# Retention of the later segments with one row half of TensorE for each half of the heads, and q loaded in two layouts

## The chip, the cores and the metric

The kernel runs on one core of a Trainium2 chip. Its engines are TensorE (PE in the profile; its weight loads are the row PEld), VectorE (DVE), ScalarE (ACT), GpSimd (POOL) and SyncE (SP). SP issues nearly all DMA transfers of this kernel, in order, and 16 DMA engines carry them out. The metric is the device time of one execution in microseconds (us), lower is better; a time is the median of several runs.

## The reference

Retention (a linear attention whose state decays) is followed by a feed-forward block with a gate. There are 4 batch elements, 8 heads of width 64 and 768 time steps; the rows go on as 3072 tokens of width 512, the hidden width is 1536, and all is float32.

```python
gamma = 1.0 - 2.0 ** (-5.0 - np.arange(H))
for t in range(S):
    state = gamma * state + np.einsum('bhd,bhe->bhde', k[:, :, t], v[:, :, t])
    y[:, :, t] = 1 / np.sqrt(D) * np.einsum('bhd,bhde->bhe', q[:, :, t], state)
x = y.transpose(0, 2, 1, 3).reshape(B * S, H * D)
g = x @ w_gate
out = (g * sigmoid(g) * (x @ w_val)) @ w_out
```

## The kernel before

**Segments.** The 3072 tokens are worked in four segments of 768: three chunks of 128 steps of two batch elements each. Segments 0 and 1 are the two halves of the first two batch elements, 2 and 3 of the other two. A segment has three parts: retention, the up products (gate and value, with the gate's activation), and the down product. Segment 0 has its retention at the start (L633 to L744), and its up products (L937, L919) run while the weights arrive and are converted. From segment 1 on the up products (`product`, L1088) need 7 block products in place of 8 (a Strassen-like scheme with sums of x and of the weights).

**Split operands.** Large products run on a fast matmul format that holds fewer bits, so each operand is split in three terms. `near_a` (ACT), `near_b` (DVE) and `near_c` (POOL or DVE) split weights and the hidden values; `far_a`, `far_b`, `far_c` split x and the down weights of segment 0. In the plan `w` steps split the up weights, `h` steps the hidden values, `d` steps the down weights of segment 0, `x` steps the inputs of the up products, after four sums (`sum`) on DVE.

**Stage of interest.** `down_stage` (L1199) runs the down products of segment s: 72 pieces D, one for each of the 12 hidden blocks and 6 token blocks, each of three matmuls 128x512 (L1157), adding up in PSUM banks 0 to 5, one bank for each token block. Between them stands the retention of segment s+1, made of small 64x64 float32 matmuls, all issued by one helper (`mm`, L789). Such a matmul uses a quarter of PE's array: a row half (which 64 partitions the operands lie on) and a column half (which 64 partitions of PSUM it writes). A pair p is one chunk position of both batch elements (c = 0, 1), and z counts the two halves of 64 steps of a chunk. For each pair there are four groups:

- sc: the scores of keys and queries (`scores_of`); DVE multiplies them with the decay mask (`decayed`, L812) into `att`.
- A: `low` (scores times v) and half of `old` (queries times the earlier state) for z = 0, and `grow`, which makes what the 64 steps add to the state.
- B: the rest of `old` for z = 0, and `low` and half of `old` for z = 1.
- C: the rest of `old` for z = 1, and `grow` for z = 1.

In `low`, `old` and `grow` the row half belongs to a batch element and alternates with z. Scores of pair 0 use banks 4 and 5, all else banks 6 and 7 (R0 = 6). The state is kept on DVE (`keep_state`, L894) after ACT has multiplied the old one by its decay (`decay2`, L888). ACT scales k (`scale_k2`, L824), DVE and POOL scale q in place (`scale_q2`, L816 and L401), and ACT copies the result y to `chunk_x`, eight copies of 64x128 for each z (`bring_y`, L1022). From there the sums and the splits of x for the next up products are made.

**Loads.** `load_pair` (L783, L786) brings k and q with the head's width on partitions and v and k with time on partitions, 256 KB for each batch element, to places in the tile `loads`, which the up weights (`load_unit`, L1060) use as well. `w_load` (L1133, L1136) brings the down weights. The output is scaled and stored by `finish` (L1184 to L1187).

**Order.** Nothing is scheduled by a compiler. `PLAN` is a list of steps written out, and each engine runs its instructions in the order of that list; semaphores hold a step until what it reads is there. The times in `at(...)` only matter for steps that the list does not name.

Of the kernel before, what the change touches and what calls it, by code (L numbers as in the profile page):

```python
# [17 lines left out]
P = 128  # L18
# [33 lines left out]
    A0 I0 l0:0 l1:0 A2 A1 U0:0 s0 a0:1 r1 l0:2 s1 b0:1 A4 A3 l2:1 l2:0 r0 m0 K0 S0:1 c0:1 l1:2 x0:1  # L52
    t0 s2 E1 l3:0 l3:1 m1 l2:3 C0:1 g2 V0:0 a0:0 Q2 n0:0 b0:0 l2:2 x1:2 s3 x1:1 n0:1 l4:1 l4:0 l3:2
    t1 S0:0 k2 x0:2 q3 c0:0 C0:0 o2 U1:1 m2 o3 n0:3 s4 m3 a1:1 n0:4 x2:1 l5:1 l3:3 b1:1 x2:2 x3:1
    S1:1 t2 n0:2 p0:0 q4 a1:0 x3:2 c1:1 n0:5 k3 C1:1 g3 b1:0 n1:0 v0:0 l5:0 U2:3 s5 S1:0 t3 c1:0
    C1:0 l5:2 p0:1 n1:1 u0:0 u0:1 T0:0 q5 v0:1 a2 l4:2 b2 y0:1 o5 y0:0 o4 n1:3 S2 n1:2 m5 T0:1 n1:4
    c2 m4 n1:5 x5:2 p1:0 l5:3 x5:1 p1:1 u1:0 C2 v1:0 U3:1 T0:2 x4:2 T1:0 U12:0 a3 v1:1 y1:0 x4:1
    T1:1 L b3 p0:2 a12 c12 n2:0 S3 u1:1 T1:2 b12 u0:2 U4:3 c3 Z0 n2:1 v0:2 Z1 n2:3 S12 y1:1 a4 n2:2
    p1:2 v1:2 C3 u1:2 n2:4 G2:0 y0:2 C12 G2:1 n3:0 U13:1 y1:2 n3:1 n2:5 b4 T2:0 n3:2 S4 U5:2 n3:3
    c13 T2:1 W2:0 Z12 W2:1 h0 c4 i2:1 n3:4 i2:0 G3:0 n3:5 T3:0 C4 T2:2 T3:1 U6:3 j2:0 a5 G3:1 T3:2  # L60
    j2:1 Z2 n4:0 U7:0 W3:0 i3:0 n4:1 b5 n4:2 n4:3 S5 n4:4 W3:1 i3:1 n4:5 c5 G4:0 C5 n5:0 a6 b6 a13
    l4:3 T4:0 j3:0 G4:1 n5:1 j3:1 Z3 T4:1 n5:3 i4:0 n5:2 T4:2 S6 W4:0 b13 c6 i4:1 n5:4 a7 S13 C6
    W4:1 n6:0 T5:0 U8:2 Z4 b7 U14:3 n5:5 n6:1 G5:0 j4:1 S7 C13 j4:0 G5:1 n6:2 a8 n6:3 P2 n6:4 i5:1
    c14 W5:1 i5:0 Z13 c7 j5:1 T6:0 n6:5 W5:0 a14 U9:1 U15:0 C7 T5:1 G6:0 T6:1 n7:0 T5:2 G6:1 n7:3
    n7:1 T6:2 i6:0 b8 j5:0 Z5 S8 n7:4 W6:1 b14 g4 n7:2 G7:0 i6:1 W6:0 P0 c8 S14 C8 Z6 C14 h2 a9 b9
    G7:1 j6:1 n7:5 S9 n8:0 c15 n8:3 j6:0 k5 c9 W7:1 Z14 T7:0 n8:1 C9 n8:4 U10:2 a15 n8:2 i7:1 U11:1
    W7:0 T7:1 j7:1 n8:5 i7:0 T8:0 T7:2 b15 Z7 S15 a10 n9:0 G8:0 G8:1 W8:1 i8:0 n9:3 b10 j7:0 T8:1
    n9:1 n9:2 U16:3 S10 a11 n9:4 G9:0 k4 i8:1 t4 C15 c10 C10 n9:5 W8:0 g5 n10:0 T8:2 T9:0 b11 c16
    n10:1 G9:1 Z15 j8:0 j8:1 n10:2 a16 n10:3 t5 U17:2 b16 W9:0 i9:1 T9:1 0/h0.0 T9:2 S11 Z8 W9:1 S16
    G10:1 n10:4 i9:0 C16 c11 C11 n10:5 n11:0 j9:0 Z9 G10:0 n11:3 Z16 i10:1 j9:1 a17 i10:0 W10:1 P1  # L70
    n11:4 T11:0 T11:1 1/was0.0 T11:2 n11:1 W10:0 Z11 c17 n11:2 n11:5 b17 0/h0.1 0/W0 G11:1 0/h1.0
    G11:0 j10:0 0/d0.0 h1 0/h0.2 1/sc0 j10:1 i11:0 0/h1.1 0/W1 S17 0/d1.0 i11:1 0/d0.1 1/l3 C17
    T10:0 1/dec0.0 W11:0 0/d1.1 0/d0.2 W11:1 0/h2.0 j11:0 0/D0.2 j11:1 1/k0.0 1/l4 1/dec0.1 1/q0.0
    0/D0.1 1/q0.1 0/D0.4 1/k0.1 1/l5 0/D0.0 0/h2.1 0/d1.2 0/h1.2 0/h4.0 0/W2 0/Z0 1/A0 1/y0.06
    1/new0.0 0/h4.1 1/y0.01 0/D0.5 0/D0.3 0/d2.0 1/B0 0/D1.1 0/h3.0 1/y0.03 0/D1.5 1/y0.04 0/Z1
    1/y0.02 1/y0.07 1/y0.05 T10:1 1/was0.1 1/y0.15 1/y0.00 1/y0.14 0/d2.1 0/D1.4 1/y0.12 0/d2.2
    0/D1.2 1/y0.13 0/W3 Z17 0/D1.3 0/Z2 0/d3.0 0/D1.0 0/h2.2 0/h3.1 1/C0 0/W4 T10:2 0/h3.2 0/d3.1
    0/h4.2 Z10 1/y0.16 1/l7 1/y0.17 1/new0.1 1/sum0.0 0/D2.3 0/D2.1 1/y0.10 0/h5.0 1/begin 1/sum0.1
    0/d3.2 0/h5.1 1/y0.11 0/D2.5 1/sc1 0/D2.0 0/d4.0 1/was1.0 0/D2.4 0/d4.1 0/D3.4 1/l6 1/dec1.1
    0/h5.2 1/dec1.0 0/D2.2 1/x0.2.0 0/D3.1 1/q1.1 0/d4.2 0/W5 0/D3.5 1/x0.1.0 0/h6.0 1/k1.0 0/Z3  # L80
    1/sum0.3 1/k1.1 1/sum0.2 1/x0.2.1 0/D4.5 0/D3.2 0/D3.3 0/D3.0 1/q1.0 0/Z4 0/h6.1 0/D4.0 0/D4.4
    1/x0.1.2 1/x0.1.1 1/A1 1/x0.0.0 0/d5.0 1/x0.2.2 1/y1.00 0/h6.2 1/y1.06 1/x0.0.2 1/new1.0 0/D4.2
    0/d5.1 0/d5.2 0/D4.3 0/D4.1 1/y1.07 1/y1.01 0/W6 0/h7.0 1/B1 1/x0.0.1 1/y1.04 1/y1.12 0/h7.1
    1/l9 0/d6.0 0/D5.4 0/h8.0 0/d6.1 1/y1.02 0/D5.3 0/D5.2 0/W7 0/h8.1 1/y1.05 0/d6.2 1/l8 1/l11
    0/Z5 1/y1.03 1/was1.1 0/D5.5 1/C1 0/d7.0 1/y1.16 0/d7.1 0/D6.5 0/D5.0 1/y1.17 1/y1.15 1/new1.1
    0/h7.2 1/y1.14 1/y1.11 0/D5.1 1/y1.13 1/x1.2.0 0/D6.3 0/d7.2 0/D6.4 0/Z6 1/y1.10 0/D7.3 0/h9.0
    1/sc2 0/h8.2 1/x1.2.2 0/D6.2 1/q2.1 1/k2.1 0/D7.5 0/W8 1/sum1.0 0/D6.1 1/sum1.2 1/k2.0 0/D6.0
    0/D7.1 1/x1.1.0 0/h10.0 0/h9.1 0/d8.0 0/D7.2 1/dec2.0 1/l10 1/sum1.1 1/dec2.1 0/W9 1/x1.1.1
    0/D7.0 0/d8.1 1/x1.2.1 0/Z7 1/sum1.3 1/was2.0 1/q2.0 1/x1.0.0 1/x1.1.2 0/d9.0 0/D7.4 0/d8.2
    0/h11.0 1/A2 1/new2.0 0/D8.0 1/x1.0.1 0/h10.1 0/D8.3 0/D8.2 0/d9.1 1/L0 0/D8.1 1/y2.00 0/D8.4  # L90
    1/B2 0/W10 0/d9.2 1/y2.07 1/y2.05 0/d10.0 0/D8.5 0/h9.2 1/y2.02 0/h11.1 0/D9.3 1/y2.03 0/h10.2
# [279 lines left out]
def tile_retnet_swiglu(  # L371
# [314 lines left out]
    def keep_rows():  # L686
        copy(tab[:, QDEC0:KDEC0], banks[2])
# [652 lines left out]
```

## Time and profile before

| what | value |
|---|---|
| median of 3 runs | 642.69 us (641.97 to 642.97) |
| profiled execution, first to last instruction | 640.5 us |
| retention of segment 0 and first up products | 0 to 46 us |
| up products of segment 0 | 46 to 127 us |
| down of 0 with retention of 1 | 127 to 197 us |
| up of 1; down of 1 with retention of 2 | 197 to 282; 282 to 350 us |
| up of 2; down of 2 with retention of 3 | 350 to 435; 435 to 503 us |
| up of 3; down of 3 | 503 to 589; 589 to 637 us |
| small matmuls (L789) in the chain | 6.0% of the span |
| granted clock of TensorE | 1.000 |

The span is the profiled execution's own time from its first to its last instruction; what a run needs around it is the difference to the median. A group row of the profile gives line, engine, operation, the tiles written and read, shapes and count, then the busy time and the mean of one in ns, then the engine's idle time just before such instructions and what ended it. The chain is followed back from the last instruction to what released each.

### The profile page before, as it was taken

Reading aid. Unit: us, or ns where it says so; the run is one execution under the profiler, and the core shown is the slowest. Engines: PE = TensorE matmul, PEld = TensorE weight load, DVE = VectorE, ACT = ScalarE, POOL = GpSimd, SP = SyncE. Lnnn points to the kernel's source line nnn. Section 1 sums busy time; section 2 is a strip of 40 time slices with the busy share of each in tenths; the row PEclk is TensorE's granted clock in tenths of the full one; section 3 lists DMA queues with packets and bytes.
Section 4 is the critical chain, followed back from the end, with each engine's and each line's share of the span. In section 5 each row is a group of like instructions: output and inputs, shape, how many; then the busy total and the mean of one; then the engine's idle time right before and its main releaser. Section 6 shows DMA issues by size and latency. Waiting matters only on the chain.

```text
span 640.5 us, 14132 instructions
## 1 busy us (share of the span) xinstructions
PE 632.9 (99%) x5587; PEld 580.4 (91%) x5587; DVE 484.1 (76%) x715; ACT 394.3 (62%) x868; POOL 261.1 (41%) x172
## 2 busy tenths in 40 slices
PE   7999999999999999999999999999999999999997
PEld 6899999987779999997778999998777999999886
DVE  4998787899898887665797869575789866768361
ACT  4787797777865565566766555564785555654221
POOL 1534445544425866630003665550101666663000
PEclk9999999999999999999999999999999999999999
DMA  9899998798787445258765640457776444304564
GB/s 320 291 332 326 376 329 269 268 326 305 266 285 278 168 148 173 75 179 260 247 239 214 211 152 15 175 196 246 226 258 248 154 164 173 116 1 151 194 214 148
DMA packets 50626, 139.60 MB, mean 218 GB/s; under 512 B 5120, under 2 KB 18176, under 8 KB 50560
## 3 DMA queue, kind: packets, MB, share of 16 engines
q1 hardware_dynamic: 49984, 137.92, 62.6%
q8 instruction: 44, 0.72, 0.5%
q10 hardware_dynamic: 576, 0.79, 0.3%
q14 instruction: 22, 0.18, 0.1%
HBM read 108.80 MB, written 29.88 MB: 217 GB/s over the span
## 4 chain that ended last, share of the span: by engine, by line
PE 97%; DMA 3%; SPq 0%; DVE 0%; ACT 0%; issue 0%
PE bank L1088 41%; PE bank L1157 32%; PE bank L919 13%; PE bank L789 6%; PE bank L937 3%; DMA hT<-in_v_n_dram 2%; PE bank L744 1%; DMA hT<-in_q_t_dram 1%; PE bank L730 0%; PE bank L715 0%; PE bank L633 0%; DVE chunk_x L1178 0%; SPq L513 0%; ACT chunk_x L1180 0%; SPq L466 0%
## 5 line engine op out<-in xcount | busy, mean ns | idle before, releaser
L1157 PE MATMUL bank<-oitem,gitem 128*128 128x512 f32 x867 | 208.2, 394 | 0.0
L1157 PEld LDWEIGHTS bank<-oitem,gitem 128*128 128x128 f32 x867 | 159.6, 188 | 34.5 <-DVE tmp L812 0.4
L997 POOL TENSOR_TENSOR gitem<-gitem 128x768 fp32r<-128x768 f32 x71 | 138.7, 1963 | 117.9 <-DVE gitem L994 99.0
L1088 PE MATMUL bank<-xa,gitem 128*128 128x384 f32 x864 | 160.5, 334 | 0.0
L1088 PEld LDWEIGHTS bank<-xa,gitem 128*128 128x128 f32 x864 | 150.8, 188 | 0.2
L997 POOL TENSOR_TENSOR oitem<-oitem 128x256 fp32r<-128x256 f32 (+1 forms) x60 | 64.1, 1074 | 56.8 <-DVE oitem L994 48.3
L1088 PE MATMUL bank<-xb,gitem 128*128 128x384 f32 x432 | 84.5, 334 | 0.0
L919 PE MATMUL bank<-xa,oitem 128*128 128x384 f32 x480 | 84.3, 335 | 0.0
L919 PEld LDWEIGHTS bank<-xa,oitem 128*128 128x128 f32 x480 | 83.0, 188 | 0.4 <-ACT tmp L444 0.2
L994 DVE SCALAR_TENSOR_TENSOR gitem<-gitem,loads 128x768 fp32r<-128x768 f32 x72 | 75.1, 1057 | 9.1 <-ACT gitem L991 7.5
L1088 PEld LDWEIGHTS bank<-xb,gitem 128*128 128x128 f32 x432 | 75.9, 188 | 0.4
L991 ACT ACTIVATE gitem<-loads 128x768 fp32r<-128x768 f32 x72 | 59.6, 843 | 26.0 <-PE bank L1088 16.8
L994 DVE SCALAR_TENSOR_TENSOR gitem<-gitem,hT 128x768 fp32r<-128x768 f32 x48 | 46.1, 965 | 24.4 <-ACT gitem L991 24.4
L991 ACT ACTIVATE gitem<-hT 128x768 fp32r<-128x768 f32 x48 | 40.2, 842 | 31.4 <-PE bank L1157 29.4
L1022 ACT COPY chunk_x<-bank 64x128 f32<-64x128 f32 x144 | 36.6, 260 | 32.6 <-PE bank L789 21.3
L401 DVE SCALAR_TENSOR_TENSOR gitem<-gitem 128x768 fp32r<-128x768 f32 x49 | 49.7, 1022 | 1.3 <-DVE gitem L994 0.5
L816 POOL TENSOR_TENSOR loads<-loads,tab 128x512 f32<-128x512 f32 x9 | 13.4, 1493 | 82.1 <-PE bank L789 44.6
L1088 PE MATMUL bank<-xb,oitem 128*128 128x384 f32 x216 | 43.4, 335 | 0.0
L1088 PEld LDWEIGHTS bank<-xb,oitem 128*128 128x128 f32 x216 | 37.9, 188 | 0.3
L994 DVE SCALAR_TENSOR_TENSOR oitem<-oitem,loads 128x256 fp32r<-128x256 f32 (+1 forms) x42 | 34.5, 824 | 2.1 <-ACT oitem L991 2.1
L1105 DVE TENSOR_TENSOR hT<-bank,tmp 128x384 f32<-128x384 f32 x36 | 20.0, 555 | 20.7 <-PE bank L1088 20.4
L1103 ACT COPY tmp<-bank 128x384 f32<-128x384 f32 x36 | 17.2, 478 | 28.3 <-PE bank L1088 19.3
(118 smaller groups left out, 789.8 us busy)
## 6 DMA issues: line engine op xcount, KB each, us to landing
loads<-wup SPq DMA_DIRECT2D x36, 896.0 KB, 4.7
oitem<-wdnt SPq DMA_DIRECT2D x33, 768.0 KB, 4.4
wdnt<-oitem SPq DMA_DIRECT2D x12, 768.0 KB, 5.5
wup<-first SPq DMA_DIRECT2D x9, 896.0 KB, 6.7
rawp<-in_w_gate_dram SPq DMA_DIRECT2D x12, 512.0 KB, 6.8
rawp<-in_w_val_dram SPq DMA_DIRECT2D x12, 512.0 KB, 6.2
rawp<-in_w_out_dram SPq DMA_DIRECT2D x12, 512.0 KB, 5.7
out_dram<-chunk_x SPq DMA_DIRECT2D x21, 256.0 KB, 2.1
```

The costliest lines, as they stand in the source:

```text
L401: stt(o, x, 1.0, y, op0=mul, op1=op)
L789: nc.tensor.matmul(o, a, b, start=start, stop=True, skip_group_check=True)
L919: nc.tensor.matmul(o, w[:, a, ts(b, P)], X0[:, a, i, NC - 1 - b], start=a == b == 0, stop=a == 2 and b == NC - 1, skip_group_check=True)
L937: nc.tensor.matmul(o, w[:, a, ts(b, P)], X0[:, a, :, NC - 1 - b, ts(j, P)], start=a == b == 0, stop=a == 2 and b == NC - 1, skip_group_che ...
L991: act(o[0], x, AF.Copy, scale=CUT / FAR)
L994: stt(o[1], f32(o[0]), -FAR, x, op0=mul, op1=add)
L997: op(o[2], f32(o[0]), f32(o[1]), op=add)
L1022: copy(cx[half[i], ds(2 * h, 2), c, half[z]], y.rearrange("p (b t) -> p b t", b=2))
L1088: nc.tensor.matmul(o, w[:, a, k], x[:, a, KH - 1 - k], start=start and a == k == 0, stop=a == 2 and k == KH - 1, skip_group_check=True)
L1103: steps = (lambda: copy(p1, x), lambda: tt(c11, z, p1, op=add), lambda: act(gate, c11, AF.Silu, scale=ONE), lambda: copy(u2, x), lambda: c ...
L1105: lambda: copy(p5, wb), lambda: tt(h1, x, p5, op=add),
L1157: nc.tensor.matmul(banks[tok][:, cols], hs[f][:, a, ds(i * TH + u * P, P)], wo[f][:, a, cols], start=f == a == 0, stop=f == NF - 1 and a = ...
```

## The change

The row half now belongs to half of the heads (g = 0: heads 0 to 3, g = 1: heads 4 to 7) for `low`, `old` and `grow`, for both batch elements and both z. For this, v and k with time on partitions are loaded so that a row half holds 64 partitions of its four heads, both z side by side: four transfers of 64 partitions for each, in pieces of 1 KB. q is loaded twice: as before for the scores, and a fifth load of a pair (`w` = 4) for `old`, to the place that k of the scores had; DVE scales that copy, with a table that two transfers bring (`own_rows`). With this the products of one z stand in one group (`mix2`), so B holds what B and C held, and C is gone: three groups for a pair. The result of `grow` for the second batch element lies on the other row half, and ACT copies it over (`move_state`; `turn_state` once, for the state from segment 0). y now leaves PSUM in two copies of 128x256 for each z. k is scaled by ACT alone. The scores of pair 1 use banks 4 and 5.

A set ELSE names 45 steps that go to another engine than by default: 32 additions of the up weights' split and six of the down weights' split go from POOL to DVE, one stays on DVE, and six steps that scale the output change between ACT and DVE. The store of an output tile is a step of its own (`store`). The list is the same for its first 150 steps and in another order behind them; loads and steps of the retention stand in it by name. In the order of PE the small matmuls of segment 1 stand at: scores of 0, A0, scores of 1, B0, A1, B1, scores of 2, A2, B2; in segments 2 and 3 the scores of pair 1 follow A0 at once.

```diff
+    def either(step):
+        return both if step in ELSE else pool
...
-    spots = [loads[:, ts(i, 512)] for i in range(10)]
-    HOME = (2, 3, 4, 0, 1, 2, 3, 4, 0, 1, 4, 0)
+    homes = [loads[:, ts(i, 1024)] for i in range(5)]
+    homes += [chunk_x[:, ts(1, 1024)], tmp[:, ts(1, 1024)]]
+    HOME = (2, 3, 4, 5, 2, 0, 1, 3, 6, 0, 1, 4, 5, 0, 1)
...
     def load_pair(s, n):
+        p, w = divmod(n, 5)
+        t = homes[HOME[n]]
+        given.setdefault(p, {})[w] = [t[:, ts(c, 512)] for c in range(2)]
+        one, two = seg_chunks(s)[2 * p], seg_chunks(s)[2 * p + 1]
+        src = (k_t, q_t, v_n, k_n, q_t)[w][one : two + 1 : two - one]
+        if w < 2:
+            nc.sync.dma_start(out=two_of(t), in_=src.rearrange("c r n -> r c n"))
+            return
+        for c in range(2):
+            for g in range(2):
+                nc.sync.dma_start(
+                    out=two_of(t[half[g], ts(c, 512)]),
+                    in_=src[c, :, ts(g, 256)].rearrange("(z t) n -> t z n", z=2))
...
     def scores_of(p, own):
+        scored[p] = own
         kt, qt = ([pairs(t) for t in given[p][w]] for w in range(2))
+        for z in range(2):
+            for b in range(2):
                 for c in range(2):
+                    for g in range(2):
+                        for i in range(2):
+                            mm(banks[own + i][half[g], ds(256 * c + 128 * z + HC * b, HC)],
+                               kt[c][half[i], 2 * g + b, half[z]],
+                               qt[c][half[i], 2 * g + b, half[z]], z == b == c == 0)
     def decayed(p, i):
-        att[p, i] = (spare if p % 2 else tmp)[:, ts(i, 512)]
-        o, b = (t.rearrange("p (z n) -> p z n", z=2) for t in (att[p, i], scored[p][i]))
-        tt(o, b, lmask[:, i][:, None, :].to_broadcast([P, 2, NP * HC]), op=mul)
-    def scale_q2(p, i):
-        t = pairs(given[p][1][i])
-        (pool if i else both)(t, t, qdec, op=mul)
-    def scale_k2(p, i):
-        kd = given[p][3][i].rearrange("p (h d) -> p h d", h=H)
-        if p == 2 and i == 0:
-            pool(kd, kd, lk[:, :, None].to_broadcast([P, H, D]), op=mul)
-            return
-        for h in range(H):
-            act(kd[:, h], kd[:, h], AF.Copy, scale=lk[:, ds(h, 1)])
...
+    def state_of2(z, c, g):
+        return moved[half[g]] if c else states[half[g], z, g]
+    def move_state(z):
+        for g in range(2):
+            copy(moved[half[g]], states[half[1 - g], z, g])
+    def turn_state(i, g):
+        for c in range(2):
+            copy(states[half[g ^ c], 1, g].rearrange("p (b i) e -> p b i e", b=2)[:, :, i],
+                 states[half[i], 0, c, ds(2 * g, 2)])
+    def y_at(z, c, g, b, i):
+        return banks[R0 + g][half[i], ds(256 * z + 128 * c + HC * b, HC)]
     def low(p, z):
         for b in range(2):
+            for c in range(2):
+                for i in range(2):
+                    for g in range(2):
+                        mm(y_at(z, c, g, b, i),
+                           given[p][2][c][half[g], ds(256 * z + D * (2 * b + i), D)],
+                           att[p, i][half[g], ds(256 * c + 128 * z + HC * b, HC)], b == c == 0)
+    def old(p, z):
+        for b in range(2):
+            for c in range(2):
+                for i in range(2):
+                    for g in range(2):
+                        mm(y_at(z, c, g, b, i), state_of2(1 - z, c, g)[:, 2 * b + i],
+                           given[p][4][c][half[g], ds(256 * i + 128 * b + HC * z, HC)])
     def grow(p, z):
         for n in range(NP):
+            for c in range(2):
+                for g in range(2):
+                    own = ds(256 * z + D * n, D)
+                    mm(banks[R0 + g][half[g ^ c], ds(256 * (1 - z) + D * n, D)],
+                       given[p][3][c][half[g], own], given[p][2][c][half[g], own])
+    def mix2(s, p, z):
+        low(p, z)
+        if has_old(s, p, z):
+            old(p, z)
+        if has_new(s, p, z):
+            grow(p, z)
+    def decay2(z, g):
         for n in range(NP):
+            act(states[:, z, g, n], states[:, 1 - z, g, n], AF.Copy,
+                scale=lg[:, ds(NP * g + n, 1)])
...
-    def bring_y(z, h, i, c):
-        y = banks[R0 + c][half[h], ds((2 * z + i) * 2 * HC, 2 * HC)]
-        copy(cx[half[i], ds(2 * h, 2), c, half[z]], y.rearrange("p (b t) -> p b t", b=2))
+    def bring_y(z, r):
+        y = banks[R0 + r][:, ts(z, 256)].rearrange("p (c b t) -> p b c t", c=2, b=2)
+        copy(cx[:, ds(2 * r, 2), :, half[z]], y)
...
-        at(t + c, f"{s}/w{f}.{g}.2", lambda: near_c(it["o"][0], both if (s, f, g) == (1, 0, 0) else pool))
+        at(t + c, f"{s}/w{f}.{g}.2", lambda: near_c(it["o"][0], either(f"{s}/w{f}.{g}.2")))
...
-            at(t + b, f"{s}/d{f}.1", lambda: far_b(o(), f32(o()[2]), pool))
+            at(t + b, f"{s}/d{f}.1", lambda: far_b(o(), f32(o()[2]), either(f"{s}/d{f}.1")))
...
-        if tok % 2:
+        if (tok % 2 == 1) != (f"{s}/e{tok}" in ELSE):
             nc.vector.tensor_scalar(t, banks[tok], scale, None, op0=mul)
         else:
             act(t, banks[tok], AF.Copy, scale=scale)
-        nc.sync.dma_start(out=out[ds(row, P)], in_=t)
...
+            at(t, f"{nxt}/begin", begin_x, nxt)
             for f in range(3):
-                at(slot_at[UNITS[f]], f"{nxt}/L{f}", load_unit, f)
+                at(t, f"{nxt}/L{f}", load_unit, f)
+            for n in range(15):
+                at(t, f"{nxt}/l{n}", load_pair, nxt, n)
+            for i in range(4 if nxt == 1 else 0):
+                at(t, f"{nxt}/cv{i}", turn_state, i // 2, i % 2)
+            if nxt == 1:
+                at(t, f"{nxt}/cm", move_state, 1)
+            for p in range(L):
+                at(t, f"{nxt}/sc{p}", scores_of, p, 6 if p == 2 else 4)
+                for i in range(2):
+                    at(t, f"{nxt}/dec{p}.{i}", decayed, p, i)
+                    at(t, f"{nxt}/q{p}.{i}", scale_q2, p, i)
+                for n in range(NP):
+                    at(t, f"{nxt}/k{p}.{n}", scale_k2, p, n)
+                for z in range(2):
+                    at(t, f"{nxt}/{'AB'[z]}{p}", mix2, nxt, p, z)
+                    if has_new(nxt, p, z):
+                        for g in range(2 if has_old(nxt, p, z) else 0):
+                            at(t, f"{nxt}/was{p}.{z}{g}", decay2, z, g)
+                        at(t, f"{nxt}/new{p}.{z}", keep_state, nxt, p, z)
+                        at(t, f"{nxt}/mv{p}.{z}", move_state, z)
+                    for r in range(2):
+                        at(t, f"{nxt}/y{p}.{z}{r}", bring_y, z, r)
+                make_x(t, nxt, p, table)
```

## Prediction

> **What bounds the kernel now.** I read the busy shares first, then the chain that ended last in order of time, then busy time by stage, then the groups on VectorE (DVE) and GpSimd (POOL) inside one stage, then the transfers. A stage below is the stretch from the first small matmuls for segment 1, 2 or 3 to that segment's up products: 127 to 197, 282 to 350 and 435 to 503 us.
>
> ```profile
> span 640.5 us, 14132 instructions
> ...
> PE 632.9 (99%) x5587; PEld 580.4 (91%) x5587; DVE 484.1 (76%) x715; ACT 394.3 (62%) x868; POOL 261.1 (41%) x172
> ```
>
> TensorE (PE) is busy for all but 7.6 us, and those lie ahead of the first 20 us and behind the last matmul, where the change touches nothing. So the time is what PE's rows add up to: a step helps only if it shortens PE's own row, and hurts only if PE comes to wait. In the chain, each piece is start, length, line and number of records (a 64x64 fp32 matmul leaves two records, a 128x512 one leaves one):
>
> ```profile
> 146.84 1.09 PE bank L789 x64
> 147.94 8.39 PE bank L1157 x36
> 156.32 1.34 PE bank L789 x80
> 157.67 2.27 PE bank L1157 x9
> 159.93 1.09 PE bank L789 x64
> 161.02 2.95 PE bank L1157 x12
> 163.97 0.86 PE bank L789 x48
> ...
> 175.92 1.52 PE bank L789 x80
> 177.43 3.66 PE bank L1157 x15
> 181.09 1.40 PE bank L789 x64
> ...
> 185.48 0.39 PE bank L789 x16
> ```
>
> Two things are to be seen. From 16 to 64 records a small run grows from 0.39 to 1.09 us, 0.0146 us a record, so 0.156 us of each run is there whatever its size. Behind a small run the down products cost (8.39 - 2.27) / 27 = 0.227 us each, and 2.27 - 9 x 0.227 = 0.23 us more. **A run of small matmuls thus costs about 0.39 us for being a run.** Second, the runs at 175.92 and 181.09 are longer than their twins of the same size (1.34 and 1.09): 0.18 + 0.31 us of waiting inside them.
>
> By stage (window, length, busy time of PE, PEld, DVE, ACT, POOL, clock, DMA share, GB/s):
>
> ```profile
> 127.00:197.00 70.00, 70.00 (x981) 56.74 (x982) 64.81 (x90) 50.15 (x139) 27.14 (x18) 1.00 0.85 300
> 197.00:282.00 85.00, 85.00 (x492) 85.00 (x491) 63.77 (x98) 48.79 (x96) 56.83 (x35) 1.00 0.47 156
> 282.00:350.00 68.00, 68.00 (x974) 54.89 (x973) 51.07 (x79) 47.20 (x139) 9.96 (x6) 1.00 0.70 238
> ```
>
> Only in stage 1 is a second engine near PE: DVE with 64.81 of 70.00.
>
> **The change part by part.**
>
> *Fewer runs.* The built order of PE holds the same 4299 instructions, among them the same 1104 small matmuls, in both programs. The runs of small matmuls number 36 before (12 a stage) and 25 after (9, 8 and 8: C is gone, and in segments 2 and 3 A0 and the scores of pair 1 stand together). 11 x (0.156 + 0.23) = **4.3 us off**, all of it on the path. The records keep their price: the four 64x64 tiles are still taken in turn and each row half still keeps to its own bank; A (x80, with grow) and the scores (x64, without) fit the same 0.0146.
>
> *ACT.* Out go 144 copies of y (260 ns), 120 scalings of k (336) and 60 decays (392), 101 us by mean times count. In come 36 copies of 128x256 (376, the row of the first state's copy), 72 scalings of 128x128 (392), 120 decays of 128x64 (340, the early decay's row) and about 42 copies of state (376 at most): 98 us. ACT is 62% busy, so this costs nothing; PE hides it. Without that cover the terms cancel anyway.
>
> *POOL to DVE.* 50 additions and scalings leave POOL (the 9 of q, 3 of k, 6 of the first weights for down, 32 of the up weights); the new scaling of q, the 6 and 33 with an earlier one are on DVE. At 0.68 us for 128x512, 0.95 for 128x768 and 0.41 for 128x256 DVE gains some 36 us. In an up stage that is about 10 on 63.77 of 85: hidden. In stage 1 it is 9 x 0.68 = 6.1 us on 64.81 of 70, which would not fit, were it not for this pair of rows, the same line in two windows of that stage (127 to 141.9, then 170.2 to 186):
>
> ```profile
> L1007 DVE SCALAR_TENSOR_TENSOR oitem<-oitem 128x512 fp32r<-128x512 f32 x3 | 3.7, 1227 | 0.0
> ...
> L1007 DVE SCALAR_TENSOR_TENSOR oitem<-oitem 128x512 fp32r<-128x512 f32 x3 | 2.0, 679 | 0.0
> ```
>
> One of the first three took 2.32 us, while POOL was at a 1.77 us addition. Summed over the stage, DVE's rows are some 8.5 us above their shortest forms with 18 POOL instructions there. The change takes 10 of the 18 away, so I take 4.7 us back against 6.1 added: +1.4, which DVE's 5 us of idle time hold. I count the 0.5 us of waiting at 175.92 and 181.09 (its releasers are DVE's sums of x and splits) as **gone**, bounds 0 to 0.6.
> The Trainium skill, SBUF — State Buffer, "Who interferes with whom", says that a DVE instruction with two SBUF inputs and a GpSimd instruction that reads SBUF lock each other out for a whole instruction. The 2.32 us row agrees; by that rule DVE in stage 1 loses a wait of up to one POOL instruction (1.5 us) for each of the 10, and ends below its 64.81; by durations alone it would end at 70.9.
>
> *q loaded twice.* New on SP: 14 transfers for a pair instead of 10, and a dependence that was not there. The second layout of q goes to the place of k, so it is issued when the scores are done, and A's products with the state (`old`, L847) need it scaled. Rows, of the tile loads in stage 2 (ns least, median, most) and its issues (KB, median us to landing):
>
> ```profile
> L786 SPq DMA_DIRECT2D loads<-in_v_n_dram x4: 472/530/728, 302.7 to 322.7; - x4
> ...
> loads<-in_v_n_dram SPq DMA_DIRECT2D x4, 128.0 KB, 5.4
> ```
>
> The reload is four such half tiles (in 1 KB pieces, not 2 KB, which only the weight loads have here, 512 KB in 6.8 us; I bound the landing by 3.6 and 9.3 us, the quickest median of such halves, in stage 3, and the slowest of the tile's loads, in stage 1, and take 5.4). Last issue 1.6 us behind the scores, landed at 7.1, scaled on DVE at 7.8. Pairs 0 and 1 have over 14 us. For pair 2 the order leaves twelve, ten and fifteen down products (0.68 each) between scores and A; with the two switches and A's first 16 matmuls that is 8.9, 7.6 and 10.9 us. So in stage 2 it is late by 0.2. Behind it DVE holds three splits of x and two of h (0.35, 0.35, 1.15, 0.87, 0.87) ahead of the new state (0.72), and ACT then moves that state (0.75) for B, which stands four down products on: 13.0 against 12.3 us after the scores, **0.7 late in all**. In stage 1 the same sum gives 16.4 against 17.0, but one POOL instruction falls into it: **0.3**. Stage 3 has room. Bounds for the three: 0 and 8.
>
> *Banks and order.* Scores of pair 1 now use banks 4 and 5, which the down products of the tokens 4 and 5 need. In stage 1 two products stand between; DVE has a new state, a split and two decays to do: 6.4 against 6.65 us. I take **0.2**, bounds 0 and 1. New stores of the output wait later on SP, and the up steps of segment 0 are reordered; PE's 336 products there run at 0.174 us with no wait, and their transfers are issued within 10 us of where they were: 0.
>
> **Sum.** 640.5 - 4.3 - 0.5 + 0.7 + 0.3 + 0.2 = 636.9 us of span. The median of the runs, 642.69, is 2.2 above the span; that part lies outside it and stays: **639.1 us**.
>
> **Rivals.**
> *The reload is late by more* (12 in 100). Landing at 7.1 us, the slowest of loads in stage 2, adds 1.7 there and 0.6 in stage 1: 641.4. For it: four more issues a pair on one queue. Against: that queue mostly waits for others.
> *DVE is the bound in stage 1* (7 in 100). If fewer POOL instructions give nothing back, 64.81 + 6.1 = 70.9 us of DVE stand against 70 - 1.2 saved: 2.1 late, and the 0.5 stays: 641.7.
> *The runs do not cost what I say* (4 in 100): if the 0.39 us follows something else, such as the tile order or bank, nothing is won, and the waits give 643.4 or so.
> *Slower* (7 in 100). One mechanism: the reload behind the scores of pair 2. At the slowest landing, 9.3 us, q is scaled at 11.7 us after the scores, against 8.9, 7.6 and 10.9: 2.8, 4.1 and 0.8 late, 0.7 more at B: 8.4 us of waiting for 4.8 won, **646 us**. It decides from a landing of about 8 us on; the DMA share of 0.85 in stage 1 speaks for it, 0.70 in stage 2 less.
> *All is hidden* belongs to the forecast (70 in 100 with it): without any new wait 637.9, with 0.41 for a run 637.6.
>
> **Chances.** A measurement can tell about 0.2%, 1.3 us, from no change. Faster: the forecast and most of the first rival, 0.81. Same: the rest of it and DVE as the bound, 0.11. Slower: 0.08. The range reaches from 637.2 (no waits, dearer runs) to 642.4, past DVE as the bound.
>
> **What would show it.** 25 pieces of small matmuls in the chain, each at 0.156 + 0.0146 a record; a longer one, or a gap, names a wait. L1007-like rows near 0.68 us in stage 1 and DVE's busy time there not above 67. In stage 2, whether A2 and B2 wait, and for which: the load of q, or the state's copy. Wrong would be PE waiting for DVE all through stage 1, or PE below 98% of the span.

## The result, and the profile after

The changed kernel took **663.42 us** (median of 5 runs, 659.97 to 666.25), the kernel before 642.84 us beside it (5 runs, 641.97 to 643.80): a ratio of 1.0308, 95% interval 1.0277 to 1.0339. It is slower by 20.6 us where 3.6 us less were forecast. The profiled run took 666.25 us, with a span of 664.1; it is the slowest of the five. In two of the experiments below (e4 and e7) one execution lay over 1.5% above the fastest of its kernel; the ratio leaves it out, the median and the text's differences hold it.

The changed kernel's page: span, busy time of the engines, and the granted clock in 40 slices, in tenths.

```profile
span 664.1 us, 14143 instructions
...
PE 642.2 (97%) x5587; PEld 589.1 (89%) x5587; DVE 495.2 (75%) x760; ACT 391.7 (59%) x815; POOL 183.8 (28%) x122
...
PEclk9999999997999979999999999999899999999999
```

PE has as many matmuls as before, yet is busy 9.3 us longer, idle 14.3 us more, and granted less than the full clock around 156, 242 and 470 us. Two kinds of loss, then: waits, and matmuls at half clock.

The changed kernel by stage (window, length, busy time of PE, PEld, DVE, ACT, POOL, clock, DMA share, GB/s). The first and third are stages 1 and 2 of the prediction, the second is the up stage between them:

```profile
127.00:207.70 80.70, 75.18 (x936) 61.48 (x936) 65.52 (x102) 51.75 (x128) 11.32 (x7) 0.96 0.88 305
207.70:294.00 86.30, 82.99 (x519) 82.36 (x518) 63.65 (x99) 47.36 (x96) 45.84 (x28) 0.96 0.43 141
294.00:366.30 72.30, 71.10 (x941) 59.39 (x940) 57.90 (x90) 48.06 (x125) 0.74 (x1) 1.00 0.73 250
```

Stage 1 is 10.7 us longer. DVE is not what filled it: 65.52 us in the longer window, against 64.81 in 70.00 before.

What PE waited for between 127 and 600 us, as the profile names it (total, times, longest):

```profile
PE bank L1160 <- DMA oitem<-wdnt: 4.6, 3, 2.0
PE bank L1091 <- ACT tmp L1106: 3.3, 1, 3.3
PE bank L798 <- ACT chunk_x L1025: 1.9, 1, 1.9
PE bank L798 <- DVE states L897: 1.3, 1, 1.3
PE bank L1160 <- ACT states L889: 1.2, 1, 1.2
PE bank L922 <- DVE hT L459: 1.1, 1, 1.1
PE bank L798 <- DVE loads L414: 0.6, 1, 0.6
PE bank L1160 <- DVE tmp L820: 0.4, 1, 0.4
...
```

Before, PE waited for nothing there but the 0.5 us inside two runs. The first row is down weights that land late. The others name no load: they name a copy out of a bank (L1106, L1025), a state, a scaling. For the longest of them the loads stand one step further back. Take the 1.9 us, at 153.1 us. SP's queue ahead of it (start, length, line, transfer, count):

```profile
142.89 3.50 SPq L793 DMA_DIRECT2D loads<-in_q_t_dram  x4
...
147.12 0.38 SPq L1136 DMA_DIRECT2D oitem<-wdn  x1
```

And ACT, where the bracket is the idle time before:

```profile
153.46 0.63 ACT L1003 ACTIVATE oitem<-oitem 128x512 fp32r<-128x512 f32 x1 [3.87 <-DMA oitem<-wdn]
153.99 0.68 ACT L831 ACTIVATE tmp<-tmp,local 128x128 f32<-128x128 f32 x2
154.58 0.62 ACT L1025 COPY chunk_x<-bank 128x256 f32<-128x256 f32 x2
```

The four issues of q's second layout (L793) hold SP for 3.50 us. The weight behind them (L1136) goes out at 147.12, ACT waits 3.87 us to split it, and the copy of y (L1025) that stands two places behind on ACT comes late, so B cannot have its bank. The weight lands 6.2 us after its issue, at 153.35, with the DMA engines full (share 1.04 from 151 to 155 us), so the late issue is one part of its lateness and the transfers ahead of it are another. The longest wait, 3.3 us at 239.1 in the up stage, has a scaling in place of the split. ACT again:

```profile
237.69 0.40 ACT L831 ACTIVATE chunk_x<-chunk_x,local 128x128 f32<-128x128 f32 x1 [3.33 <-DMA chunk_x<-in_k_n_dram]
238.98 0.40 ACT L831 ACTIVATE chunk_x<-chunk_x,local 128x128 f32<-128x128 f32 x1 [0.89 <-DMA chunk_x<-in_k_n_dram]
...
241.87 0.47 ACT L1106 COPY tmp<-bank 128x384 f32<-128x384 f32 x1
```

k lands late, so its scalings (L831) are late, and behind them in ACT's order stands the copy (L1106) that frees a bank for the up products. In stage 2, at 339.3 us, the profile puts the wait of 1.2 us down to ACT's decay of the state (L889), but the step that waits is a down product (L1160), which reads no state. Its weight is the one to look at:

```profile
329.75 3.43 SPq L793 DMA_DIRECT2D loads<-in_k_n_dram  x4
333.28 0.54 SPq L1063 DMA_DIRECT2D loads<-wup  x1
333.94 1.69 SPq L1139 DMA_DIRECT2D oitem<-wdnt  x2
```

The first of the two weights (L1139), issued at 333.94 behind k's four issues, landed at 340.38, and PE's wait for that landing ended at 340.41, 0.1 us ahead of the product. So it is a late down weight too.

**Where 23.5 us went.** In the profiled run the last matmul ends at 660.59 us, before at 637.07. Behind 20 us PE has gaps of 15.5 us in all, before none. Half clock was granted for 6.83, 6.83 and 3.41 us; PE was busy for 15.7 us of that, so some 7.9 us of work were lost. The start is 1.0 later. Less the 4.3 us of the runs that went, this makes 20.1; the 3.4 left are not put down to a row. The clock's part differs from run to run: the mean granted clock was 0.987 here and 0.994 to 0.997 in the other four, which by these figures lost some 2 to 4 us to it (an estimate).

### The profile page after: what moved, and what is told of

Read it like the earlier page. It is cut to its first block, busy times and chain, and to the rows that moved or that the text cites. A ratio compares the mean times of both kernels' runs of the same rounds, so it can differ in the third digit from the quotient of the medians.

```text
span 664.1 us, 14143 instructions
## 1 busy us (share of the span) xinstructions
PE 642.2 (97%) x5587; PEld 589.1 (89%) x5587; DVE 495.2 (75%) x760; ACT 391.7 (59%) x815; POOL 183.8 (28%) x122
## 2 busy tenths in 40 slices
DMA packets 60850, 144.59 MB, mean 218 GB/s; under 512 B 5872, under 2 KB 33008, under 8 KB 60784
## 4 chain that ended last, share of the span: by engine, by line
PE 58%; DMA 4%; ACT 1%; SPq 0%; issue 0%; DVE 0%; ACTq 0%
PE bank L1091 35%; PE bank L1160 19%; DMA oitem<-wdnt 3%; PE bank L798 3%; DMA loads<-in_k_n_dram 0%; SPq L793 0%; ACT loads L831 0%; ACT states L889 0%; ACT gitem L994 0%; DVE chunk_x L1183 0%; ACT tmp L1106 0%; ACT bank L1107 0%; ACT chunk_x L1185 0%; ACT bank L1110 0%; ACT xb L1003 0%
## 5 line engine op out<-in xcount | busy, mean ns | idle before, releaser
L1160 PE MATMUL bank<-oitem,gitem 128*128 128x512 f32 x867 | 209.0, 398 | 6.2 <-DMA oitem<-wdnt 4.6
L1160 PEld LDWEIGHTS bank<-oitem,gitem 128*128 128x128 f32 x867 | 163.0, 191 | 43.0 <-DMA oitem<-wdnt 2.4
L1091 PEld LDWEIGHTS bank<-xa,gitem 128*128 128x128 f32 x864 | 152.9, 191 | 4.0 <-ACT tmp L1106 3.6
L1000 POOL TENSOR_TENSOR gitem<-gitem 128x768 fp32r<-128x768 f32 x48 | 96.3, 2016 | 175.1 <-DVE gitem L997 154.0
L1000 POOL TENSOR_TENSOR oitem<-oitem 128x256 fp32r<-128x256 f32 (+1 forms) x51 | 56.1, 1103 | 167.8 <-DVE oitem L997 149.8
L1091 PE MATMUL bank<-xb,gitem 128*128 128x384 f32 x432 | 81.8, 335 | 0.0
L414 DVE SCALAR_TENSOR_TENSOR gitem<-gitem 128x768 fp32r<-128x768 f32 x72 | 71.2, 994 | 1.9
L1107 ACT COPY tmp<-bank 128x384 f32<-128x384 f32 x36 | 17.2, 477 | 36.0 <-PE bank L1091 20.1
L889 ACT ACTIVATE states<-states,local 128x64 f32<-128x64 f32 x120 | 31.5, 335 | 1.5 <-DVE states L897 1.5
L1025 ACT COPY chunk_x<-bank 128x256 f32<-128x256 f32 x36 | 12.4, 367 | 30.4 <-DVE states L897 16.1
L1108 ACT COPY tmp<-bank 128x384 f32<-128x384 f32 x36 | 17.3, 480 | 14.1 <-PE bank L1091 14.0
```

Source lines behind the costliest of these rows:

```text
L414: stt(o, x, 1.0, y, op0=mul, op1=op)
L889: act(states[:, z, g, n], states[:, 1 - z, g, n], AF.Copy, scale=lg[:, ds(NP * g + n, 1)])
L1000: op(o[2], f32(o[0]), f32(o[1]), op=add)
L1025: copy(cx[:, ds(2 * r, 2), :, half[z]], y)
L1091: nc.tensor.matmul(o, w[:, a, k], x[:, a, KH - 1 - k], start=start and a == k == 0, stop=a == 2 and k == KH - 1, skip_group_check=True)
L1107: lambda: act(gate, c11, AF.Silu, scale=ONE), lambda: copy(u2, x),
```

## The experiments

The changed kernel is the base unless another is named; "before" is the kernel before on the same chip. **T1**: the time goes on SP's queue, in the four issues of every half-tile load, because what stands behind them, the down weights and the scalings of k and q above all, no longer fits the places that the list gives it. **T2**, the rival: the moves from POOL to DVE overload DVE. **T3**, named in the expectations from e2 on: the new list puts steps ahead of others that are due sooner, whatever the transfers cost.

**1. e1_else_off: POOL keeps its steps.**

```
-ELSE = {"0/d1.1", ... "3/w8.1.2"}
+ELSE = set()
```

> The set ELSE is empty, so 38 splits of weights go back from DVE to POOL and six scalings of the output change back between ACT and DVE; the loads, the retention and the list of steps stay those of the changed kernel (663.4 us). Theory 1 (in-order queues: the retention's half-tile loads hold SP, the down weights behind them come late, and ACT's and DVE's scalings that wait for a load hold other steps; the clock then falls to half): the gaps of PE at 153, 239, 339, 468 and 496 us stay, so 660 to 667 us, rather more than less since POOL locks DVE out again. Theory 2 (the 38 steps given to DVE overload it): most of the loss goes, 640 to 650 us, and DVE's busy time falls by about 25 us.

672.68 us, before 642.31: 1.0453 (1.0415 to 1.0491). The kernel gets 9 us slower without the moves, and PE's longest waits now end on POOL (6.8 us in three). T2 falls: the moves help. T1's 660 to 667 us were exceeded as well.

**2. e2_one_issue: one transfer a load.**

```
-        if w < 2:
+        if w < 5:
```

> v, k with time on partitions and the second q are each brought by one transfer of 512 KB in rows of 2 KB, not by four of 128 KB in pieces of 1 KB; same bytes, same places, same waits and same list. The data do not lie as the products need them, so the numbers computed in the retention differ. Theory 1: SP is free 2 to 3 us sooner behind each of the 27 loads, the down weights come sooner, and the gaps of PE of 15.5 us fall to under 6 and the half clock to under 4 us: 640 to 650 us. Theory 3 (the new list puts steps ahead of others that are due sooner, whatever the transfers cost): no gain, 660 to 666 us. Theory 2: no gain either.

648.21 us (646.94 to 652.75): 1.0100 (1.0062 to 1.0139); gaps 6.7 us, clock 1.000. With the same bytes, list and instructions 15 us are back, and no half clock is left behind the start. The weight of the gap at 153 us now goes out at 144.09, 3.0 us sooner, and lands at 149.74, 3.6 sooner. T1 holds; T3 by itself, which said no gain, falls.

**3. e3_no_reload: q's second load left out.**

```
+        if w == 4:
+            return
```

> The second load of q is left out (nine loads of four transfers), and the products of queries and the earlier state use what lies in that place (keys), so the numbers computed differ; the scaling on DVE and all else stays. If the second load of q alone is at fault (the prediction's slower rival): all gaps go, 637 to 641 us. Theory 1: the gaps where a down weight stands behind a q load on SP (468, 496 us) and the one at 187 us go, those of k behind its own wait (239, 339 us) and of the down weight behind the load at 143 us stay at least in part: 648 to 658 us. Theory 3: 660 us or more.

652.21 us: 1.0145 (1.0120 to 1.0170), gaps 9.2 us. The reload with its four issues is worth 11 us, though A and B wait little for it by name.

**4. e4_weights_first: weights ahead of the loads, twelve moves in the list** (`0/W2 > 1/l8`, `0/W3 > 1/l9` and so on).

> Twelve loads of down and up weights are put ahead of the retention's load that stood in front of them in the list, so SP issues them first; the same work. Theory 1: PE no longer waits for down weights (gaps at 153, 468, 496 and 517 us, 6.5 us and half clock twice, some 4 us), while the waits for k scaled on ACT at 239 and 339 us stay or grow, since the retention's loads are later by 0.5 us: 648 to 656 us. If the order on SP does not matter (theory 2): 660 to 667 us. If the retention's loads have no time to spare, the gaps only move to A and B groups: 658 to 668 us.

681.33 us: 1.0587 (1.0556 to 1.0618). Three of the moves (W7 ahead of l13 in two stages, W8 ahead of l14 in one) put a down weight into a place whose earlier weight has products later in the list, so that those products wait for the new weight and use it; that is the part of the computation it changes. PE waited 13.1 us for weights, up to 5.1 at a time. The experiment was ill made and speaks for neither side.

**5. e5_rows_2kb: still four issues, but pieces of 2 KB.**

```
-                    out=two_of(t[half[g], ts(c, 512)]),
-                    in_=src[c, :, ts(g, 256)].rearrange("(z t) n -> t z n", z=2))
+                nc.sync.dma_start(out=t[half[g], ts(c, 512)], in_=src[c, half[g]])
```

> The four transfers of 128 KB of each half-tile load stay, each with 64 partitions, but each row is one piece of 2 KB and not two of 1 KB: the same number of issues and bytes, half as many packets. The data do not lie as the products need them, so the numbers computed in the retention differ. If it is the small pieces that make the loads dear (on SP or in the DMA engines): most of what one transfer for each load gave (663.4 to 648.2 us) comes back, 646 to 654 us, and an issue is shorter than 0.6 us. If it is the number of issues in a row on SP: 658 to 666 us, four issues still 2.5 us.

661.91 us, before 642.72: 1.0309 (1.0281 to 1.0337), gaps 14.4 us. The small pieces (33008 packets under 2 KB in the changed kernel, 19184 here, 18176 before) are not at fault. With e2, it is the number of transfers for a load: their issues, their landings, or both.

**6. e6_z_form: four transfers over 128 partitions, the two halves as first dimension.**

```
+            for z in range(2):
...
+                    out=t[:, ds(512 * c + 256 * z, 256)],
+                    in_=src[c, ts(z, 64)].rearrange("t (g n) -> g t n", g=2))
```

> Each half-tile load is cut the other way: four transfers of 128 KB, each over all 128 partitions and one half of 64 steps, in pieces of 1 KB. Same bytes, same pieces, same layout, same count. Theory 1 (the issue's time on SP): it depends on whether an issue over 128 partitions is shorter; the 512 KB loads over 128 partitions take 0.43 us, so four would take 1.7 in place of 2.6 us: 655 to 662 us. If the pieces' landing decides, no change: 660 to 667 us.

880.99 us: 1.3706 (1.3684 to 1.3727). The issues (count, then least, median and most in ns):

```profile
L793 SPq DMA_DIRECT2D loads<-in_q_t_dram x36: 506/2491/5987, 127.1 to 701.8; - x36
```

DVE waited for these loads 82.7 us in 15 times, and where only these transfers ran, some 50 GB/s were moved at a busy share of one tenth, where 300 to 400 GB/s are seen beside that. The Trainium skill, DMA: Bandwidth & Descriptors, "Why a DMA increments its semaphore by 16 and not by 1", says that the number of DMA engines used is the largest up to 16 that divides the slowest dimension of both sides; here that is 2. The measurement agrees. For the question it is a miss: the form was worse than the one it replaced.

**7. e7_pool_queue: the half tiles issued from POOL** (`nc.sync.dma_start` becomes `nc.gpsimd.dma_start` at L793).

> All half-tile loads are issued by POOL and not by SP; the same list. Theory 1: SP does not stand still for 2.6 us or wait for the place of a load, so the down weights behind it are on time: the gaps at 153, 468, 496 and 517 us go, 6.5 us, and with them the half clock there; but POOL now waits for the places, and its splits behind that wait are late, DVE's and ACT's waits for k and q stay: 650 to 660 us. If SP's queue is not what delays: 661 to 668 us.

679.04 us: 1.0556 (1.0528 to 1.0583). POOL in order of time, and the wait of PE that comes of it:

```profile
126.09 2.35 POOL L793 DMA_DIRECT2D loads<-in_q_t_dram  x4
128.45 1.31 POOL L1000 TENSOR_TENSOR oitem<-oitem 128x512 fp32r<-128x512 f32 x1
129.67 4.71 POOL L793 DMA_DIRECT2D loads<-in_v_n_dram  x8
```

```profile
PE bank L922 <- DVE hT L459: 7.8, 1, 7.8
```

An issue takes 0.59 us on POOL too, and now holds POOL's splits. DVE is held in turn: the scaling of q that it began at 133.56, 0.68 us long by itself, took 3.80 us beside POOL's work, and the step that PE waited for (L459) stands two places behind it. Moving the issues to another queue that has work moves the stall.

**8. e8_moved: nine places of the list mended**, each weight or load that a gap named moved ahead (`0/W3 > 1/l9`, `0/W9 > 1/L1`, `2/W2 > 3/l9` and so on).

> Only the list is changed, in nine places, by PE's gaps of the changed kernel: five down weights (W3 and W9 of the first, W7 of the second, W2, W5, W7, W9 of the third stage; seven in all) stand ahead of the load that held them up on SP, wherever the products that free their place stand earlier, and ACT's scalings of k0 in the second up stage and of k2 in stage 2 stand later. Theory 3 (the list's order does not fit the transfers' times): the gaps at 153, 239, 339, 468, 496 and 517 us go, 11 us, with the half clock of 7 us twice: 644 to 652 us. If the gaps only move to the loads that now come later: 655 to 668 us.

662.85 us: 1.0311 (1.0278 to 1.0344), gaps 15.8 us. Of the six gaps that were aimed at only the one at 239 us went. The other five are there again within 4 us of their places, that at 152 us with DVE's state ahead of the copy of y in place of the weight, and gaps of 1.8 and 1.7 us have come at 180 and 275 us. Single moves did not mend the list.

**9. e9_laid_out: one transfer a load, with the data in its right layout.** Three more inputs hold v, k and q in the half-by-half order, prepared with the inputs and outside the time, so that the load needs no four parts:

```
+        src = (k_t, q_t, v_g, k_g, q_g)[w][one : two + 1 : two - one]
+        nc.sync.dma_start(out=two_of(t), in_=src.rearrange("c r n -> r c n"))
```

> The rows that the half-tile loads put together are laid out so in the inputs (three more arrays: k, v and q by halves of the heads; the other arrays of k, q, v, too, come permuted), so that every load is one transfer of 512 KB in rows of 2 KB over 128 partitions, with the data that the products need. The list is that of the changed kernel. Theory 1 (the four issues of a load hold SP): the same as with one transfer and the wrong rows, 646 to 650 us, clock 1.0, no gap of PE over 1.1 us. If the numbers themselves mattered (wrong rows cheaper): over 655 us.

648.63 us (645.33 to 652.27), before 643.18: 1.0084 (1.0046 to 1.0123), gaps 6.5 us. It agrees with e2, now with the whole computation. The issues of q's second layout in the changed kernel, and in e9:

```profile
L793 SPq DMA_DIRECT2D loads<-in_q_t_dram x32: 595/598/1350, 142.9 to 492.5; - x32
```

```profile
L791 SPq DMA_DIRECT2D loads<-in_q_g_dram x8: 368/376/1203, 141.2 to 471.9; - x8
```

Four of 0.60 us became one of 0.38. But with 11 runs fewer this kernel should have been at 643.18 - 4.3 = 638.9: 10 us are still missing.

**10. e10_before_split: the kernel before, with 16 issues for a pair in place of 10.**

```
+                n = 64 if i == 0 else 32
+                for m in range(0, P, n):
+                    nc.sync.dma_start(out=own[i][m : m + n],
+                                      in_=src[ds((m + 64 * i) % P, n)])
```

> The kernel before, with 16 issues for a pair in place of 10: the four 256 KB loads of v and k with time on partitions are cut in halves or quarters by partitions, same bytes and rows of 2 KB. That adds some 3.3 us of issuing for a pair on SP, about what the changed kernel adds (10 issues at 0.5 us against 14 at 0.6). Theory 1 in its plain form (time on SP is lost to PE in any order): PE waits in each of the three stages, 646 to 655 us. Theory 3 (the new list and the fifth load leave no room, the list of before does): 642 to 645 us.

648.23 us, before 643.18: 1.0067 (1.0038 to 1.0096), with gaps of 5.1 us where there were none. Issues alone take 5 us from a kernel whose list had no waits. They do not take 20: the list has a part in that. The down weights landed as in the kernel before (768 KB in a median of 4.6 us, against 4.5, from 127 to 600 us), so here it is SP's time.

**11 to 13. e11_fit_after, e12_fit_laid, e13_fit_early: the list put together anew** from the durations in the traces, by a count of what each engine, bank and queue has to do: e11 for the changed kernel's loads and e12 for those of e9, from step 378 on; e13 for those of e9 from step 186 on. Only `PLAN` differs.

> The changed kernel with the same steps on the same engines, the same loads (four transfers of 128 KB for a half-tile load) and the same places; only the list behind its first 377 steps is put together anew, from the durations that the traces of the changed kernel show, with 0.62 us for an issue over 64 partitions, 2 to 3.4 us and 300 to 360 GB/s for a landing. Theory 3 (the list's order against the transfers' times is at fault, there is room enough): PE's gaps behind 130 us fall from 13.5 to under 4 us and the half clock goes, 638 to 646 us. Theory 1 in its strict form (SP has no room for the issues in any order): 652 us or more.

> Every load one transfer, with the inputs laid out for it (k, v and q come in one more permutation), and the list behind its first 377 steps put together anew in the same way. Both theories: the gaps behind 130 us (5 us with the old list) go, 25 runs of small matmuls stay, so 648.6 - 5 to 6: 641 to 644 us; with the 0.6 us that PE also lost in waits too short to be listed, 640. If something else than waits costs the new scheme time (PE itself): 645 us or more.

> As e12, with the list anew from its 186th step on, so with the conversions and first up products of segment 0 as well. The gaps at 85 and 131 us (1.9 us with the old list) go too, 24 runs of small matmuls: 1.5 to 3 us less than e12, 637 to 641 us, at or below the forecast of 639.1. If the conversions of the weights have no room (DVE and POOL locking each other out): no less than e12.

671.45 us, 1.0449 (1.0428 to 1.0471); 667.77 us, 1.0384 (1.0367 to 1.0401); 662.51 us, 1.0305 (1.0290 to 1.0321). Three misses, all worse than the list they replaced. e12's splits on DVE (count, least, median, most in ns), and two waits of its stage 1:

```profile
L410 DVE SCALAR_TENSOR_TENSOR gitem<-gitem x60: 943/957/2601, 127.0 to 593.3; 128x768 fp32r<-128x768 f32 x60
```

```profile
DVE tmp L809 <- PE bank L1149: 3.6, 1, 3.6
...
PE bank L787 <- ACT local L833: 4.2, 1, 4.2
```

They show what the count lacked. A split of 0.95 us took up to 2.60 beside a POOL instruction. DVE's decay of the scores waited 3.6 us for down products in the other of banks 4 and 5, which the kernel declares as one tile. ACT's split of x waited 4.1 us for a place that a store of weights (`wup<-first`) was still reading, and PE 4.2 us for ACT.

**14 and 15. e14_apart_laid, e15_apart_after: the list anew, with these three counted**, from step 186 on; e14 with e9's loads, e15 with the changed kernel's own half-tile loads. Part of the list around the down weights (W) and the loads (l) of stage 1, other steps left out, in the changed kernel and in e15:

```
-1/A0 1/sc1 1/l8 0/d2.0 0/h3.0 1/l9 1/k1.3 1/k1.2 0/h5.0 0/W3 0/d3.0 1/k1.1 1/B0 0/W4 1/k1.0 1/A1 1/l10 0/W5 1/l11 1/l12
+1/A0 1/sc1 0/W2 1/l8 0/d2.0 1/l9 1/k1.3 1/k1.2 1/k1.1 0/W3 0/h3.0 1/k1.0 0/d3.0 1/B0 0/h5.0 0/W4 1/A1 0/W5 1/l12 0/W6
```

> As e13 (one transfer a load, the list anew from its 186th step on, same steps, engines and places), but the list now keeps POOL's instructions apart from DVE's with two inputs in SBUF, takes every PSUM bank (4 and 5 as one) as held by one engine at a time, and leaves 3.2 us and more for a landing. Theory 3 (order): DVE's busy time comes back to 545 us or less, gaps of PE behind 45 us under 5 us, 24 runs of small matmuls, 636 to 642 us. Theory 1 in its strict form has no say here. If the order leaves no room even so (DVE, with 38 more steps, too full beside POOL): 648 us or more.

> The same kind of list for the changed kernel with its own loads (four transfers of 128 KB for each half-tile load): only the order differs from the changed kernel (663.4 us), from its 186th step on. Theory 3 (order alone): 636 to 645 us, 25 runs of small matmuls. Theory 1 (the issues of the half-tile loads hold SP in any order): 4 us or more above e14, over 645 us.

e14: 642.64 us (10 runs), before 643.01 (16 runs): 0.9998 (0.9983 to 1.0013). e15: 648.48 us (7 runs, 644.51 to 650.36): 1.0080 (1.0055 to 1.0105). Its profiled run is the fastest, with a clock of 1.000; five of the other six show 0.996 or 0.997, so half clock is not wholly gone. The time lies where T1 put it (over 645, 4 us or more above e14) and not in the 636 to 645 of order alone; yet **order alone, with the four issues kept, gives back 15 of the 20 us**, as the one transfer alone did, and both together give all of it. The two lists are not the same, so their distance of 5.8 us is the price of the four transfers a load only to that degree.

**16. e16_tail: e14 with another end of the list,** the last products and stores closer to the changed kernel's order; e14 had ended its matmuls 2.1 us earlier than before, but its span only 6.0 us after them, before 3.4.

> As e14 (one transfer a load, list rebuilt, 24 runs of small matmuls), but the last products and stores of segment 3 end as in the changed kernel, with token 2 alone at the end and its output in two halves, and the rest of the list is fitted again around that. If only e14's stores stood between the saved matmul runs and the time: the tail falls from 6.0 to 3.4 us, so 642.6 - 2.6 = 640 us, 639 to 641, about 0.4% less than the kernel before. If the saving is lost elsewhere (DVE 25 us busier than in the kernel before): 642 to 644 us.

**638.66 us** (638.03 to 642.03, 6 runs), before 643.05 (11 runs): 0.9940 (0.9920 to 0.9959), faster than both kernels, with e9's three inputs. Its page:

```profile
span 636.9 us, 13942 instructions
...
PE 629.6 (99%) x5587; PEld 581.6 (91%) x5587; DVE 499.1 (78%) x760; ACT 391.0 (61%) x815; POOL 182.4 (29%) x122
...
PEclk9999999999999999999999999999999999999999
```

Gaps of 0.87 us are left, and the clock is whole. It has 24 runs of small matmuls: 12 x 0.39 = 4.7 us for 4.4 between the medians, 2.6 to 5.1 by the interval. The arithmetic of the change is worth what was forecast; its loads and its list took that and 20 us more.

## Why the prediction was wrong, point by point

- *Fewer runs, 0.39 us each, 4.3 us off:* **right.** Where no wait or half clock falls in, the changed kernel's pieces are 1.09 us for 64 records, 1.56 for 96, 2.02 for 128, where 0.156 + 0.0146 a record gives 1.09, 1.56 and 2.02. e16 shows the gain in the time.
- *ACT costs nothing:* right in its sum (391.7 us against 394.3), wrong as cover. ACT is 59% busy and still late, because its order holds copies and states behind a split or a scaling that waits for a load.
- *POOL to DVE is hidden in stage 1:* right. The splits there take 678, 684 and 693 ns (least, median, most), DVE's busy time is 65.5, under the 67 named, and e1 shows that without the moves the kernel loses 9 us more. The Trainium skill's rule that was weighed there (SBUF — State Buffer, "Who interferes with whom") agrees better than durations alone: by the rule DVE was to end below 64.81 us, by durations at 70.9, and 66.2 was taken; 65.52 was measured, in a longer window. The row that it was weighed by was read amiss: the split of 2.32 us began beside POOL's instruction of 2.82 us (L557, to 130.74), not beside the addition of 1.77 us, which began at 130.68.
- *0.5 us of waiting inside two runs goes:* too small to be told apart beside 15.5 us of new gaps.
- ***q loaded twice: 0.7 us in stage 2, 0.3 in stage 1, bounds for the three stages 0 and 8:* this is the step that failed.** Its waits by name were small, though not where they were put: in stage 1 A2 waited 0.57 us for the scaled q and B2 1.30 for the new state (0.3 taken), in stage 2 neither waited more than 0.14 (0.7 taken). But "14 transfers for a pair instead of 10" were priced only by the wait of A and B for their own load, and the first rival set them aside with "that queue mostly waits for others". Each issue holds SP for 0.60 us, four in a row for 2.5 to 3.5, and SP's queue carries the down weights as well. The step should have counted its own issues against what is queued behind them: the weights on SP, and behind those the splits on ACT, the copies of y, the scalings and the copies out of banks. e2 and e9 price that at 15 us, e3 at 11 for the reload alone, e10 at 5 for a list that had no waits.
- *Banks and order: 0.2, bounds 0 and 1, and the reordering 0:* the bank wait was 0.4, but **the 0 for the order failed too**: with the same loads another order is worth 15 us (e15 against the changed kernel).
- *Nothing was said of the clock:* some 7.9 of the 23.5 us of the profiled run, 2 to 4 us of the others. The prediction had "the time is what PE's rows add up to", at one clock, and a wait of 1.89 us in the wrong place costs more than itself (see the last section).
- *The rivals:* the late reload (641.4) and the slower one (646) had one of the loads at fault (e3) and the wrong victim: they let A and B wait for it; DVE as the bound fell; that the runs do not cost what was said fell. "PE below 98% of the span" was named as the sign of a wrong forecast, and it is 97%.

What stays open: what the 3.4 us without a row are, and how the price of four transfers divides between SP's time and later landings. The down weights of 768 KB took a median of 5.9 us from issue to landing in the changed kernel and 6.0 in e5, but 5.0 in e2 and 5.3 in e9 (127 to 600 us); apart from e10, no run changed the one without the other.

## What to carry to other kernels

Where an order is written out by hand and the bound engine has no idle time, price a new load by its issues in the queue and by everything behind them on that queue and on the engines that wait there in order, not by whether its own reader is late. Look for the form that loads a tile in one transfer, if need be by another layout in memory (which was prepared outside the time here), and expect to put the order together anew: either one alone gave back 15 us here, and only both together, with the end mended too, made the change a gain. An engine that is 60% busy is no cover when its instructions stand in order behind one that waits.

## What the runs showed of the hardware

**The clock falls after about half a window of idle time.** The changed kernel around its first such place (window, length, busy time of PE, PEld, DVE, ACT, POOL, clock, DMA share, GB/s):

```profile
153.00:155.00 2.00, 0.11 (x2) 0.02 (x1) 0.07 (x1) 1.54 (x5) 0.84 (x1) 1.00 1.04 434
155.00:157.00 2.00, 1.82 (x54) 1.42 (x58) 1.54 (x3) 1.59 (x5) 0.43 (x1) 0.72 0.99 391
157.00:159.00 2.00, 2.00 (x56) 1.79 (x50) 1.45 (x3) 1.22 (x4) 0.00 (x0) 0.50 1.05 415
...
161.00:163.00 2.00, 2.00 (x6) 1.53 (x6) 0.92 (x3) 1.22 (x3) 0.00 (x0) 0.57 0.03 8
163.00:165.00 2.00, 2.00 (x10) 1.65 (x9) 2.00 (x6) 1.73 (x5) 0.00 (x0) 1.00 0.67 172
```

PE waits 1.89 us from 153.1 on and then runs at half clock from 155.9 to 162.7, that is 6.83 us, or two windows of 3.413. The half clock's three beginnings lie 25 and 67 such windows apart. Over the 18 profiled runs, behind the first 20 us, the 38 windows at full clock in which PE was idle for 0.54 or more of the window were all followed by half clock, of the 16 with 0.47 to 0.54 five were, and of those with less none; a gap of 2.24 us in e15 that fell across two windows (0.41 and 0.24 idle) was followed by none. The Trainium skill, TensorE: Matmul & The Clock Gate, "What's actually happening", has these windows of 3413 ns, free-running, which agrees; under "Why this matters for your kernels" it advises against idle gaps over about 3 us, and here 1.9 us were enough.

**How long POOL holds DVE can be counted.** Over the 18 traces, a DVE instruction with two inputs in SBUF that started beside a POOL instruction ended, in the median, 0.28, 0.55, 0.82 or 1.08 us (256, 512, 768, 1024 wide; 291, 153, 434 and 13 cases) after that instruction's end: its own duration less 0.13. One with an input in PSUM took 0.550 us (384 wide) with and without POOL beside it.

**An issue has a price by its shape:** on SP, by the medians, 0.60 us for 64 partitions in two pieces, 0.38 to 0.43 for 512 KB over 128 partitions, 0.32 for 768 KB of down weights. Single issues took longer, up to 1.49 us among those of L793 in the changed kernel; those over 0.9 us were all made with two or more transfers still to land.
